# Chunk-selected attention with a routed MoE on one core: Q and K in token order, diagonal tiles masked by fours, SBUF copies by DMA

## The chip, the cores and the metric

One core of a Trainium2 chip runs the whole program in one launch. The metric is device time in microseconds; the kernel before was run three times. The engines are named as in the profile: PE (TensorE matmul), PEld (its weight loads), DVE (VectorE), ACT (ScalarE), POOL (GpSimd), SP (SyncE, which here only issues DMAs).

## What is computed

Attention over 4 batches of 8 heads, 768 tokens, head dimension 64, followed by a mixture of experts over the 3,072 tokens that come out of it. A query sees only six chunks of 32 keys: those with the largest upper bound of its score, which is worked out from the elementwise minimum and maximum of each chunk's keys.

```python
k_min = np.min(k_chunks, axis=3); k_max = np.max(k_chunks, axis=3)
ub = np.sum(np.maximum(q[..., None, :] * k_min, q[..., None, :] * k_max), axis=-1)
ub = np.where(pos[:, None] // chunk >= np.arange(nc)[None, :], ub, -1e9)
top_chunks = np.argsort(ub, axis=-1)[..., -6:]
mask = (key's chunk is in top_chunks) & (pos[:, None] >= pos[None, :])
attn = softmax(where(mask, 0.125 * q @ k.T, -1e9)) @ v
# then, on x = attn as [3072, 512]:
y_dense = relu(x @ w1_dense) @ w2_dense
expert = argmax(x @ w_gate); gate = softmax(x @ w_gate)[expert]
out = y_dense + gate * (relu(x @ w1[expert]) @ w2[expert])
```

All 8 experts have D = F = 512. The inputs are float32; the kernel works in float16 with float32 accumulation.

## The kernel before, in words

**Pairs.** The 32 heads are worked as 16 pairs p of two heads (g = 0, 1), so that the two head dimensions of 64 fill 128 partitions. The token order is interleaved: inside each block of 256 tokens, partition i of slot j holds token 2i + j (the pattern `(T p j) d` in `load`, line 84). So a "tile of 128" holds every second token of a block of 256, and all of K, Q, V and the intermediate x stay in this order.

**Preparation of a pair**, one to three pairs ahead of its use:
- `load` (L84): SP issues two DMAs of 192 KB each for K, Q and V, rows of 512 bytes.
- `cast_qk`, `cast_v` (L351, L352, L358): POOL converts to float16. Q goes into the middle half of a tile `q16` of 256 columns.
- `prep_k`: six PE transposes (L364), ACT copies the result out of PSUM as `kp` (L367), DVE takes for max and min a pairwise operation on the two slots (L372) and a reduction (L373), copies the two halves of `kp` into `kT` of each head (L374, L375), and builds `kb` (L377), the chunk bounds of both heads side by side.
- `prep_q`: six transposes (L384), ACT writes the positive part `qp` (L386), DVE the negative part `qn` (L388).
- `prep_ub`: 13 small matmuls (L393, L397) add up the bounds, twelve MAX8 operations on DVE (L403) find the sixth largest, and one comparison (L405) writes flags of the chunks that were not chosen into the outer columns of `q16`.
- `prep_s(p, g)`: per head six transposes (L411) of Q beside its flags, and a DVE copy (L413). The result `r` has, in 128 rows, the 64 of Q and the flag rows; `kT` has the 64 of K and, in the rows that meet the flags, the constant `exf`, -30000 where a key belongs to that chunk (L129). One score matmul therefore gives q.k plus a large negative number for keys of chunks not chosen.

**Scores and AV.** A head's causal scores are cut into six units of 512 columns (`PIECES`, L180): key tile by query tiles, blocks of 256 tokens on the diagonal kept whole. So a pair has 12 units and 48 tiles of 128 x 128. `scores` runs one or two matmuls (L421), ACT takes the exponential (L425), and POOL sets the entries above the diagonal to zero in the units that touch it (L430, ten of the twelve). `av` multiplies each tile with V and a column of ones (L450); `norm` (L458, L460) divides and writes x into `xbig`.

**Order.** A loop over all (pair, unit) runs scores two units ahead and AV one behind, and at fixed unit numbers the preparation of the following pairs: `prep_s` of the next pair at units 0 and 2, `prep_k` of the one after at 4, `prep_q` at 6, `prep_ub` at 9. Each engine executes its own queue in order; a tile framework inserts the semaphore waits and settles the final order in each queue. From the fifth pair on, the gate, the ranks and the dense layers of the batch before are filled in between (`batch_fills`, L212): transposes of x (L221), gate (L229), dense layers (L299, L308), stores of the dense result to DRAM (L313), of x (L248). POOL also issues the loads of the expert weights (L177) in this loop.

**Routing.** `digits` (L278, L279) writes for each tile of tokens two one-hot matrices, one with the block number of the token and one with its place in it; 48 matmuls (L589) collect them into a list of tokens by expert block. Five small DVE operations turn this into the gather index `gi` and the scatter index `si`. After attention the last batch's dense layers run, and then 31 blocks of 128 tokens: gather by POOL (L625), transposes, two expert layers (L652, L669), scatter (L673).

Of the kernel before, what the change touches and what calls it, by code (L numbers as in the profile page):

```python
# [17 lines left out]
def kernel(  # L18
# [36 lines left out]
    xov = xo.rearrange("(T p j) w -> p T j w", p=128, j=2)  # L55
    NX = 4
    xdv = xd.rearrange("(T p j) w -> p T j w", p=128, j=2)
# [16 lines left out]
    def load(p, names="kqv"):  # L74
        if p >= NP:
            return
        b, hp = divmod(p, HP)
        for nm, src in (("k", k), ("q", q), ("v", v)):
            if nm not in names:
                continue  # L80
            f = aload.tile([128, 2, NT, D], FP, name=nm + "f")
            st[p][nm] = f
            for g in range(2):
                nc.sync.dma_start(out=f[:, g].rearrange("p (T j) d -> p T (j d)", j=NJ),  # L84
                                  in_=src[b, 2 * hp + g].rearrange("(T p j) d -> p T (j d)", p=128, j=NJ))
# [7 lines left out]
    NB = 3  # L93
    kT = [[acst.tile([128, S], HF, name=f"kT{i}_{g}") for g in range(2)] for i in range(NB)]
    q16 = [acst.tile([128, NT, 256], HF, name=f"q16_{i}") for i in range(NB)]
    v16 = [acst.tile([128, 2, NT, D + 1], HF, name=f"v16_{i}") for i in range(NB)]
    for i in range(NB):
        nc.vector.memset(q16[i][:, :, 0:64], 0.0)
        nc.vector.memset(q16[i][:, :, 192:256], 0.0)
# [3 lines left out]
    nc.vector.memset(hmask[0:64, 0, :], 1.0)  # L103
    nc.vector.memset(hmask[64:128, 1, :], 1.0)
    for i in range(NB):
        nc.vector.memset(v16[i][:, :, :, D : D + 1], 1.0)
# [4 lines left out]
    exf = acst.tile([32, S], HF)  # L111
    nc.vector.memset(exf, -30000.0)

    for g in range(2):
        nc.gpsimd.affine_select(out=cbias[:, :, g, :], in_=cbias[:, :, g, :], compare_op=ALU.is_ge,
                                fill=-60000.0, base=0, pattern=[[256, NT2], [1, NJ], [-32, NC]], channel_multiplier=2)
    pat = [[256, NT2], [1, NJ], [2, 128]]
    npat = [[-a, n] for a, n in pat]
    nc.gpsimd.affine_select(out=exf, in_=exf, compare_op=ALU.is_ge, fill=0.0,
                            base=0, pattern=pat, channel_multiplier=-32)  # L120
    nc.gpsimd.affine_select(out=exf, in_=exf, compare_op=ALU.is_ge, fill=0.0,
                            base=31, pattern=npat, channel_multiplier=32)
    for i in range(NB):
        for g in range(2):
            nc.vector.memset(kT[i][g][64 * g : 64 * g + 64], 0.0)

    def expand(i):
        for g in range(2):
            nc.scalar.copy(kT[i][g][64 * g : 64 * g + 32, :], exf)  # L129
# [7 lines left out]
    Am = const.tile([128, NM, 2, 128], HF)  # L137
# [5 lines left out]
    iop = const.tile([128, NJ], FP)  # L143
    xbig = [const.tile([128, NT, XW], HF, name=f"xbig{i}") for i in range(2)]

    def route_consts():
# [11 lines left out]
        nc.gpsimd.iota(iop, pattern=[[1, NJ]], base=0, channel_multiplier=2, allow_small_or_imprecise_dtypes=True)  # L158
# [15 lines left out]
    def load_expert(e, w, behind):  # L174
# [5 lines left out]
    PIECES = [  # L180
        [(0, 0, 512)],
        [(1, 0, 512)],
        [(0, 512, 768), (1, 512, 768)],
        [(2, 256, 768)],
        [(3, 256, 768)],
        [(4, 512, 768), (5, 512, 768)],
    ]
    units = [(g, pc) for g in range(2) for pc in PIECES]
    NU = len(units)
    last_of = {}  # L190
    for u, (g, pc) in enumerate(units):
        for kt, a, z in pc:
            for t in range(a // 128, z // 128):
                last_of[g, t] = (u, kt)

# [16 lines left out]
    def batch_fills(b):  # L212
# [12 lines left out]
        def gate():  # L225
# [20 lines left out]
            for dst in (xov, xdv[:, :, :, 2 * Dm :]):  # L246
                for j in range(NJ):
                    nc.sync.dma_start(out=dst[:, b * NT2 : (b + 1) * NT2, j],  # L248
# [478 lines left out]
```

## Time and profile before

| | |
|---|---|
| median of 3 runs | 308.63 us (308.63, 308.63, 310.03) |
| profiled execution | 308.44 us, its span 306.7 us, granted clock 0.96 |
| start (first V x P matmul with a mask) | about 21.7 us |
| attention, to the last norm | 193.5 us |
| last dense layers and routing | to about 215 us |
| expert blocks | to the end |

A row of the groups reads: line, engine, operation, output and input tile, shapes, count; then the busy time in us and the mean duration of one in ns; then how long the engine stood idle just before, and what ended most of that. Busy time is the union over a group, so that overlapping matmuls are not counted twice. In the slices each digit is the busy share of a fortieth of the span in tenths. The DMA share adds up the time that packets took over 16 DMA engines; it can exceed 1 where packets of several queues overlap.

DMA issues, median from issue to landing: `kf` 4.7 us, `qf` 4.5, `vf` 5.0 (32 DMAs of 192 KB each), the stores of `ys` 3.5 (24 of 256 KB).

### The profile page before, as it was taken

Reading aid. Unit: us, or ns where it says so; the run is one execution under the profiler, and the core shown is the slowest. Engines: PE = TensorE matmul, PEld = TensorE weight load, DVE = VectorE, ACT = ScalarE, POOL = GpSimd, SP = SyncE. Lnnn points to the kernel's source line nnn. Section 1 sums busy time; section 2 is a strip of 40 time slices with the busy share of each in tenths; the row PEclk is TensorE's granted clock in tenths of the full one; section 3 lists DMA queues with packets and bytes.
Section 4 is the critical chain, followed back from the end, with each engine's and each line's share of the span. In section 5 each row is a group of like instructions: output and inputs, shape, how many; then the busy total and the mean of one; then the engine's idle time right before and its main releaser. Section 6 shows DMA issues by size and latency. Waiting matters only on the chain.

```text
span 306.7 us, 7543 instructions
## 1 busy us (share of the span) xinstructions
PE 248.3 (81%) x2607; PEld 154.7 (50%) x2607; DVE 201.2 (66%) x672; ACT 186.9 (61%) x341; POOL 194.1 (63%) x314
## 2 busy tenths in 40 slices
PE   2378877798898879898788899795939999898882
PEld 1246554476565557556566555452425544444440
DVE  6766888779997789996879952591313554443441
ACT  3658888767777987678896778232403554444440
POOL 6667988766656587467776154105764777777752
PEclk9997999989999999999999999999867999999997
DMA  7994997879996998996987821086782777777750
GB/s 198 293 290 129 208 255 147 216 126 186 264 293 162 263 194 175 304 181 157 235 149 116 239 103 70 37 297 186 208 270 93 233 244 249 231 245 255 232 188 0
DMA packets 63478, 60.75 MB, mean 198 GB/s; under 512 B 4494, under 2 KB 56718, under 8 KB 63440
## 3 DMA queue, kind: packets, MB, share of 16 engines
q0 software_dynamic: 15184, 28.60, 41.1%
q1 hardware_dynamic: 48256, 31.66, 35.5%
q8 instruction: 21, 0.34, 0.4%
q14 instruction: 17, 0.14, 0.1%
HBM read 50.62 MB, written 20.91 MB: 233 GB/s over the span
## 4 chain that ended last, share of the span: by engine, by line
PE 31%; DVE 21%; POOL 15%; DMA 12%; issue 11%; ACT 5%; SPq 2%; POOLq 1%; ACTq 0%; DVEq 0%
PE sp L421 6%; DMA xg<-xd,gi 6%; POOL xg L625 4%; PE yp L308 4%; POOL ex L430 4%; PE op L450 4%; PE yp L669 3%; DMA vf<-in_v_dram 3%; ACT ex L425 3%; DVE ks L373 3%; PE hp L652 3%; POOL out_dram L673 3%; PE hp L299 3%; DVE km L372 2%; DVE Am L279 2%
## 5 line engine op out<-in xcount | busy, mean ns | idle before, releaser
L425 ACT ACTIVATE ex<-sp 128x512 f16<-128x512 f32 x192 | 102.9, 613 | 20.4 <-PE sp L421 16.4
L430 POOL TENSOR_SCALAR_AFFINE_SELECT ex<-ex 128x256 f16<-128x256 f16 (+1 forms) x160 | 72.2, 468 | 46.3 <-ACT ex L425 43.4
L421 PE MATMUL sp<-r,kT 128*128 128x512 f16 (+1 forms) x256 | 72.7, 338 | 3.5 <-ACT ex L425 3.1
L450 PE MATMUL op<-v,ex 128*128 128x65 f16 x768 | 59.7, 197 | 6.8 <-POOL ex L430 6.5
L450 PEld LDWEIGHTS <-ex 128*128 128x128 f16 x768 | 46.0, 100 | 38.0 <-POOL ex L430 13.1
L673 POOL DMA_INDIRECT out_dram<-yo,si x31 | 31.4, 1013 | 18.1 <-DVE yo L672 13.2
L663 ACT COPY ehT<-tp 128x512 f16<-128x512 f16 x31 | 18.2, 586 | 37.2 <-PE tp L661 37.2
L646 DVE COPY exT<-tp 128x512 f16<-128x512 f16 x31 | 13.2, 425 | 37.5 <-PE tp L644 37.3
L625 POOL DMA_INDIRECT xg<-xd,gi x31 | 29.9, 963 | 11.4 <-issue 7.3
L652 PE MATMUL hp<-we,exT 128*128 x124 | 33.8, 397 | 3.3 <-issue 3.3
L669 PE MATMUL yp<-we,ehT 128*128 x124 | 33.7, 396 | 0.8 <-ACT ehT L663 0.8
L672 DVE SCALAR_TENSOR_TENSOR yo<-yp,xg 128x512 f32<-128x512 f32 x27 | 20.3, 751 | 13.6 <-PE yp L669 13.2
L655 ACT ACTIVATE eh<-hp 128x512 f16<-128x512 f32 x31 | 18.5, 597 | 15.9 <-PE hp L652 15.9
L299 PE MATMUL hp<-xT,wd 128*128 128x384 f16 x128 | 26.1, 324 | 1.4 <-DVE ys L202 0.3
L301 ACT ACTIVATE hT<-hp 128x384 f16<-128x384 f32 x32 | 15.9, 497 | 17.8 <-PE hp L299 12.0
L421 PEld LDWEIGHTS <-kT 128*128 128x128 f16 x256 | 22.5, 100 | 6.7 <-issue 5.0
L308 PE MATMUL yp<-wd,hT 128*128 128x512 f16 x96 | 25.0, 378 | 0.1
L413 DVE COPY r<-pp 128x768 f16<-128x768 f16 x32 | 16.9, 551 | 8.8 <-PE pp L411 8.7
L403 DVE MAX8 m<-pp 128x8 f32<-128x24 f32 x192 | 20.3, 173 | 3.5 <-PE pp L397 3.4
L358 POOL CAST v<-vf 128x768 f16<-128x768 f32 x16 | 13.4, 840 | 11.3 <-PE op L450 7.8
L367 ACT COPY kp<-pp 128x768 f16<-128x768 f16 x16 | 12.8, 798 | 12.7 <-PE pp L364 12.7
L397 PE MATMUL pp<-kb,qp 128*128 128x48 f16 x96 | 9.4, 187 | 13.3 <-DVE kb L377 13.3
(118 smaller groups left out, 432.7 us busy)
## 6 DMA issues: line engine op xcount, KB each, us to landing
we<-in_moe_w_dram POOLq DMA_DIRECT2D x16, 512.0 KB, 7.9
kf<-in_k_dram SPq DMA_DIRECT2D x32, 192.0 KB, 4.7
qf<-in_q_dram SPq DMA_DIRECT2D x32, 192.0 KB, 4.5
vf<-in_v_dram SPq DMA_DIRECT2D x32, 192.0 KB, 5.0
xd<-ys SPq DMA_DIRECT2D x24, 256.0 KB, 3.5
xo<-xbig SPq DMA_DIRECT2D x8, 396.0 KB, 5.3
xd<-xbig SPq DMA_DIRECT2D x8, 396.0 KB, 6.3
wd<-in_moe_w_dense_dram POOLq DMA_DIRECT2D x2, 512.0 KB, 10.1
```

The lines of the kernel that those rows point to most:

```text
L299: nc.tensor.matmul(hp, wd[:, ko, j * 128 : (j + 1) * 128], xT[:, ko, g * G * 128 : (g + 1) * G * 128], start=(ko == 0), stop=(ko == NK - 1))
L308: nc.tensor.matmul(yp, hold["h"][:, j, i * 128 : (i + 1) * 128], wd[:, NK + j], start=(j == 0), stop=(j == NK - 1))
L403: nc.vector.max(out=m8[:, t, g], in_=ub[:, t, g])
L421: nc.tensor.matmul(sp[:, o : o + z - a], kT[p % NB][g][:, kt * 128 : (kt + 1) * 128], s["r", g][:, a:z], start=(o == 0), stop=True, skip_g ...
L425: nc.scalar.activation(ex, sp, AF.Exp, scale=0.125)
L430: nc.gpsimd.affine_select(out=exd, in_=exd, compare_op=ALU.is_ge, fill=0.0, base=-(pc[0][0] % NJ), pattern=[[-1, n], [1, NJ], [2, 128]], c ...
L450: nc.tensor.matmul(op[:, t * (D + 1) : (t + 1) * (D + 1)], ex[:, c : c + 128], v16[p % NB][:, g, kt, :], start=(first and n == 0), stop=(l ...
L625: nc.gpsimd.indirect_dma_start(out=dst, out_offset=None, in_=src, in_offset=bass.IndirectOffsetOnAxis(ap=gi[:, i : i + 1], axis=0))
L652: nc.tensor.matmul(hp, s["xT"][:, ko], wef[:, bass.ds(offs[i] + ko * 512, 512)], start=(ko == 0), stop=(ko == NK - 1))
L669: nc.tensor.matmul(yp, s["hT"][:, j], wef[:, bass.ds(offs[i] + (NK + j) * 512, 512)], start=(j == 0), stop=(j == NK - 1))
L672: nc.vector.scalar_tensor_tensor(o, yp, s["x"][:, Dm : Dm + 2].bitcast(FP), s["y"], ALU.mult, ALU.add)
L673: sc = nc.gpsimd.indirect_dma_start(out=out, out_offset=bass.IndirectOffsetOnAxis(ap=si[:, i : i + 1], axis=0), in_=o, in_offset=None, bou ...
```

## The change

- **Token order at the transposes.** K is loaded interleaved as before, but ACT's copy after the transposes writes it in token order. Q's transposes write token order inside half-blocks of 64: inside a tile of 128 the even tokens come first, then the odd ones. V is loaded by plain tiles of 128 tokens, in rows of 256 bytes.
- **Units.** A tile of 128 x 128 now covers 128 consecutive keys and queries, so the causal half has 21 tiles a head instead of 24. Units are rebuilt: eleven a pair, of which three consist of four diagonal tiles each, and two have three tiles.
- **Masks.** Only these three units are masked, with one operation of 512 columns each.
- **K and flags.** ACT writes K of both heads straight into `kT[1]`; SP's DMA copies head 0's half into `kT[0]`, and another DMA puts `exf` over the rows it leaves. Flags have tiles of their own (`fl`), one set of six transposes for both heads, one DVE copy `se`, and two DMAs that place 32 rows in each head's `rT`. Q is copied by DVE into `rT[0]` and by DMA into `rT[1]`.
- **Bounds.** The negative part of Q is no longer formed: min(q, 0) k_min is written as q k_min - max(q, 0) k_min, so there are 18 instead of 12 bound matmuls, and `kb` has a third part. MAX8 reads only the causal chunks and skips the first tile.
- **One slot number.** `digits` writes one matrix with one number per token, 24 matmuls instead of 48; `gi` and `si` are worked out from it.
- Stores of x are two a batch instead of four; fills of the ranks come one unit earlier.

```diff
@@ load @@
+                if nm == "v":
+                    nc.sync.dma_start(out=f[:, g], in_=src[b, 2 * hp + g].rearrange("(t p) d -> p t d", p=128))
+                else:
+                    nc.sync.dma_start(out=f[:, g].rearrange("p (T j) d -> p T (j d)", j=NJ),
+                                      in_=src[b, 2 * hp + g].rearrange("(T p j) d -> p T (j d)", p=128, j=NJ))
@@ constants @@
     def expand(i):
-        for g in range(2):
-            nc.scalar.copy(kT[i][g][64 * g : 64 * g + 32, :], exf)
+        nc.scalar.copy(kT[i][0][64:96, :], exf[0:32])
@@ PIECES @@
-        [(0, 0, 512)], [(1, 0, 512)], [(0, 512, 768), (1, 512, 768)],
-        [(2, 256, 768)], [(3, 256, 768)], [(4, 512, 768), (5, 512, 768)],
-    units = [(g, pc) for g in range(2) for pc in PIECES]
+    def of(g):
+        return [
+            [(g, i, i, i + 1) for i in range(4)],
+            [(g, 0, 1, 5)],
+            [(g, 1, 2, 6)],
+            [(g, 2, 3, 6), (g, 4, 5, 6)],
+            [(g, 3, 4, 6), (g, 0, 5, 6)],
+        ]
+    units = of(0) + [[(g, i, i, i + 1) for g in range(2) for i in (4, 5)]] + of(1)
@@ digits @@
-            nc.vector.tensor_scalar(Am[:, m, 0], io128, rf[:, t : t + 1], float(m // NJ + 1), ALU.is_equal, ALU.mult)
-            nc.vector.tensor_scalar(Am[:, m, 1], io128, rf[:, t : t + 1], iop[:, m % NJ : m % NJ + 1], ALU.is_equal, ALU.mult)
+            nc.vector.tensor_scalar(Am[:, m], io128, rf[:, t : t + 1], num[:, m : m + 1], ALU.is_equal, ALU.mult)
@@ prep_k @@
-            kp = ahead.tile([128, S], HF, name="kp")
-            nc.scalar.copy(kp, pk)
+            kp = kT[p % NB][1]
+            nc.scalar.copy(kp.rearrange("d (T p j) -> d T p j", p=128, j=NJ),
+                           pk.rearrange("d (T j p) -> d T p j", p=128, j=NJ))
             for i, op in enumerate((ALU.max, ALU.min)):
-                km = ahead.tile([128, NC, 16], HF, name=f"km{i}")
-                nc.vector.tensor_tensor(km.rearrange("d (T c) w -> d T (c w)", T=NT2), kpv[:, :, 0], kpv[:, :, 1], op)
-                nc.vector.tensor_reduce(out=ks[:, i], in_=km, op=op, axis=mybir.AxisListType.X)
-            nc.vector.tensor_copy(kT[p % NB][0][64:128, :], kp[0:64])
-            nc.vector.tensor_copy(kT[p % NB][1][0:64, :], kp[64:128])
+                nc.vector.tensor_reduce(out=ks[:, i], in_=kp.rearrange("d (c w) -> d c w", w=32), op=op,
+                                        axis=mybir.AxisListType.X)
+            nc.vector.tensor_tensor(kb[:, 2], ks[:, 1:2].to_broadcast([128, 2, NC]), nmask, ALU.mult)
+        def prep_kt(p):
+            k0, k1 = kT[p % NB]
+            nc.sync.dma_start(out=k0[0:64], in_=k1[0:64])
+            nc.sync.dma_start(out=k1[0:32], in_=exf[0:32])
@@ prep_q @@
+            pqv = pq.rearrange("d (T h j p) -> d T h j p", h=2, j=NJ, p=64)
-                nc.tensor.transpose(pq[:, t * 128 : (t + 1) * 128], q16[p % NB][:, t, 64:192], ident)
+                nc.tensor.transpose(pqv[:, t // NJ, :, t % NJ], s["q16"][:, t].rearrange("p g d -> p (g d)"), ident)
-            nc.vector.tensor_single_scalar(qn, pq, 0.0, ALU.min)
+            nc.vector.tensor_copy(r0, pq)
+            nc.sync.dma_start(out=r1[64:128], in_=r0[64:128])
@@ prep_s @@
-                nc.tensor.transpose(ps[:, t * 128 : (t + 1) * 128], q16[p % NB][:, t, g * 128 : (g + 1) * 128], ident)
-            s["r", g] = r = ahead.tile([128, S], HF, name=f"r{g}")
-            nc.vector.tensor_copy(r, ps)
+                nc.tensor.transpose(ps[:, t * 128 : (t + 1) * 128], fl[p % 2][:, t], ident)
+            nc.vector.tensor_copy(se, ps)
+            nc.sync.dma_start(out=r0[64:96], in_=se[64:96])
+            nc.sync.dma_start(out=r1[0:32], in_=se[0:32])
@@ scores @@
-            n = sum(a == (kt // NJ) * 256 for kt, a, z in pc)
-            if n:
-                exd = ex[:, 0 : n * 256]
-                nc.gpsimd.affine_select(out=exd, in_=exd, compare_op=ALU.is_ge, fill=0.0, base=-(pc[0][0] % NJ),
-                                        pattern=[[-1, n], [1, NJ], [2, 128]], channel_multiplier=-2)
+            nc.scalar.activation(ex[:, 0:o], sp[:, 0:o], AF.Exp, scale=0.125)
+            if pc[0][1] == pc[0][2]:
+                nc.gpsimd.affine_select(out=ex, in_=ex, compare_op=ALU.is_ge, fill=0.0, base=0,
+                                        pattern=[[0, 4], [1, 2], [2, 64]], channel_multiplier=-1)
@@ the loop @@
-            if u == 0 and n1 is not None:
-                prep_s(n1, 0)
             if u == 2 and n1 is not None:
-                prep_s(n1, 1)
+                prep_s(n1)
             if u == 4 and n2 is not None:
                 prep_k(n2)
-            if u == 6 and n2 is not None:
+            if u == 5 and n2 is not None:
                 prep_q(n2)
+            if u == 7 and n2 is not None:
+                prep_kt(n2)
@@ routing @@
-            for i in range(2):
-                nc.tensor.matmul(pm[:, i], Am[:, m, i], eqb[:, m], start=(m == 0 and i == 0), stop=(m == NM - 1),
-                                 skip_group_check=True)
+            nc.tensor.matmul(pm, Am[:, m], eqb[:, m], start=(m == 0), stop=(m == NM - 1))
```

At the start the three `expand` copies now come before everything else of ACT; before, one came first and the rest after the first pair's preparation. In the changed kernel the copies of L397 and L398 (K), L410 (Q), L438 and L439 (flags) are the new DMAs on SP's queue, L448 the scores, L467 the AV matmuls and L454 the masks.

## The prediction

> **What bounds it now.** I read the busy row, the slices, the windows of the attention stage, its groups, its waits, and last the DMA of the start, in that order.
>
> ```profile
> PE 248.3 (81%) x2607; PEld 154.7 (50%) x2607; DVE 201.2 (66%) x672; ACT 186.9 (61%) x341; POOL 194.1 (63%) x314
> ...
> PE   2378877798898879898788899795939999898882
> ...
> DVE  6766888779997789996879952591313554443441
> ...
> DMA  7994997879996998996987821086782777777750
> ...
> PE 31%; DVE 21%; POOL 15%; DMA 12%; issue 11%; ACT 5%; SPq 2%; POOLq 1%; ACTq 0%; DVEq 0%
> ```
>
> One slice is 7.7 us. Attention fills slices 3 to 25, the experts' stage the last twelve. The change touches the first 215 us alone. No engine is full there, and the chain of the last end changes hands between PE, DVE and POOL: a pipeline of nearly equal engines. Windows inside it (columns: length, PE, PEld, DVE, ACT, POOL busy, clock, DMA share):
>
> ```profile
> 25.00:62.00 37.00, 28.92 (x388) 19.87 (x386) 29.12 (x97) 29.34 (x55) 30.52 (x56) 0.96 0.89 184
> 62.00:160.00 98.00, 87.09 (x1118) 60.45 (x1117) 84.04 (x312) 76.76 (x146) 66.14 (x122) 0.99 0.92 208
> 160.00:193.00 33.00, 29.98 (x351) 19.23 (x350) 22.21 (x88) 24.63 (x49) 15.48 (x33) 1.00 0.52 130
> sum 168.00, PE 145.99 PEld 99.55 DVE 135.38 ACT 130.73 POOL 112.14; mean PE 48.66 PEld 33.18 DVE 45.12 ACT 43.58 POOL 37.38
> ```
>
> In the middle window PE is busy 89%, DVE 86%, and the DMA engines 0.92. There a pair of heads takes 11.2 us (K casts of POOL L351 start at 56.47 and, eight pairs on, at 146.03). Groups of 25 to 193 us:
>
> ```profile
> L425 ACT ACTIVATE ex<-sp 128x512 f16<-128x512 f32 x184 | 98.7, 613 | 18.5 <-PE sp L421 14.5 <-PE op L450 2.0 <-POOL ex L430 1.4
> L430 POOL TENSOR_SCALAR_AFFINE_SELECT ex<-ex 128x256 f16<-128x256 f16 x122 | 50.3, 422 | 33.2 <-ACT ex L425 31.9
> ...
> L450 PEld LDWEIGHTS <-ex 128*128 128x128 f16 x739 | 44.0, 99 | 33.9 <-POOL ex L430 10.6 <-issue 9.3 <-ACT ex L425 0.2
> ...
> L430 POOL TENSOR_SCALAR_AFFINE_SELECT ex<-ex 128x512 f16<-128x512 f16 x31 | 20.2, 653 | 12.3 <-ACT ex L425 10.8 <-DMA xd<-ys 0.6
> ...
> L373 DVE TENSOR_REDUCE ks<-km 128x24 f16<-128x384 f16 x28 | 14.0, 541 | 0.0
> ...
> L375 DVE COPY kT<-kp 64x768 f16<-64x768 f16 x14 | 7.1, 507 | 0.2
> ```
>
> The reader is to see that PE waits 10.6 us for masks of POOL. A second wait of PE, for `kb` at L397 (13.3 us, 13 times), ends a DVE chain that the change rewrites.
>
> ```profile
> q1 hardware_dynamic: 10413, 5.12, 99.5%
> ...
> kf<-in_k_dram SPq DMA_DIRECT2D x10, 192.0 KB, 4.8
> ```
>
> This is the DMA of the first 20 us: SP's queue keeps all 16 engines full. 0.995 x 20 us x 16 / 10,413 is 30.6 ns for a packet of 512 bytes.
>
> **The Trainium skill.** "VectorE: DVE Perf Modes", section "The perf-mode tier table": a tensor_reduce has only the one-element-a-cycle mode, at 0.96 GHz. The trace agrees: 384 elements take 541 ns, 400 of them elements, so 768 should take 941 (an estimate). "SBUF — State Buffer", section "SBUF: two separate sides": DVE and GpSimd lock a port pair from each other for a whole instruction. The trace fits: one `digits` operation (L279) took 1.90 us at 131.05, while POOL issued weights and ran masks, 0.31 us at 201 with POOL idle. "DMA: Bandwidth & Descriptors", section "Why small descriptors are slow (HBM only)": 3 cycles of overhead a packet, so 256 bytes cost 11 where 512 would cost 19; its Specifications name 512 bytes as the least for full rate. No packet of 256 bytes can be singled out here. Same page, "Queues, rings and completion order": a ring's descriptors are taken in order. So a small copy on SP's ring lands behind the loads ahead of it; landings in this trace (loads 2.3 to 9.9 us, median near 5; `ys` writes 2.0 to 7.8) are the price.
>
> **The change, step by step.** Whole-kernel counts; the sum is made against the profiled execution, 308.44 us (span 306.7), 0.19 under the median 308.63.
>
> Step 1, PE. Scores shrink from 6,144 to 5,376 columns a pair; four matmuls of 512 run in 0.86 us at L652, 0.42 ns a column: 16 x 768 x 0.42 = -5.2 us. AV matmuls 768 to 672 at 29 ns (four in 0.28 us, one 0.193): -2.8. Flag transposes 192 to 96 at 55 ns (twelve in 0.83 us): -5.3. Bound matmuls 192 to 288 at 25 ns (twelve in 0.3 us at 127.7): +2.4. Net -10.9. The Q transpose's split output I take at nothing (no row; 0 to +1 us in all).
>
> Step 2, DVE. Two `kT` copies gone, -15.2 (6.9 + 8.3). Pairwise max/min gone and reductions doubled: -13.0 + 32 x 0.40 = -0.2. Second `kb`: +16 x 0.3 = +4.8, priced as the first without contention. One flag copy of two gone: -8.5. MAX8 192 at 106 ns to 160 that are 8 columns narrower on average, 98 ns: -4.6. `digits` one of two gone, 18 before 193 us: -5.8. Net -29.5 of 135. This goes beside PE work; its worth is that PE's partners are no longer level with it. The chain from ACT's K copy to `kb` stays near 3 us (1.9 reductions, 0.55 copy, 0.7 `kb`, against 3.2 at 124.57 to 127.66), so the 13.3 us wait stays.
>
> Step 3, ACT and POOL. Exponentials 192 to 176, 32 of them of 384 columns (116 ns less, L301's 497 against 613): -12.3 of ACT. Masks 160 to 48, all of the 653 ns form: 72.2 to 31.3, -40.9 of POOL. ACT's K copy now reorders: 0 to 0.8 us each, I take 0 (same element count). Of PE's 10.6 us of waits for masks seven tenths could go, 7.4; many end with an exponential just behind, so I take -3 (0 to -7.4).
>
> Step 4, copies by DMA: five a pair on SP's queue, 344 KB, 80 in all at about 0.5 us of issue (loads' median 0.486). Per pair SP then issues 11 to 13 for about 6 us, plus one wait: `exf` into `kT` (L398) waits for the landing of the K copy just before it, and behind it stand the Q and V loads and the flag copies L438, L439. K copies are issued a pair early; loads are two pairs ahead. The flag copies are the only urgent ones: in the built order about 6.5 us of PE work lie between the flag transposes and the next pair's first score; transposing and DVE's copy take 1, so issue and landing have 5.5. With 0.5 + 4.7 they just fit, and a slower landing is late by what it exceeds. I take 0.2 us a pair, +3 in 15 pairs (0 to +8). ACT's K copy and DVE's flag copy wait for landings of two or three pairs before, long past: nothing.
>
> Step 5, V by 128 tokens: packets of 256 bytes, 1,536 a pair for 768. 17.7 ns (the page's 11/19) to 30.6: +0.23 to +1.47 us of all engines a pair, and the copies +1.2 at the start's 290 GB/s. On 10.3 us of DMA work a pair (0.92 x 11.2) that makes 11.7 to 13.0. If share meant capacity this would bind. But two queues overlap in it (the 10 to 20 us window reads 1.17, slices at 120 us reached 378 GB/s). I count nothing, and keep the rest for a rival.
>
> Step 6, start. First score now at 16.36. Two more ACT copies of `exf` lie ahead of the K copy (0.83 each): +1.7. DVE to `kb` -0.6, MAX8 -0.2, six transposes fewer and one copy fewer -1.25. Flag copy: 0.5 + 4.8 = +5.3. First score near 21.3, +4.9. But POOL's first mask waits today until 21.2 behind casts that wait for V's load; mask to mask the loss is 1.3. I take +3.
>
> Step 7, after attention. 24 of 48 slot matmuls gone (1.36 us at 205): -0.7 on a full PE; last unit needs no mask (0.65): -0.6; six `digits` operations fewer, beside PE work: -0.2. Together -1.5. Slot numbers' extra small DVE operations on `si` are hidden behind gathers; without cover 0.7. Merged `xo`/`xd` stores move the same bytes: 0.
>
> Sum: -10.9 - 3 + 3 + 3 - 1.5 = -9.4, so 299.0.
>
> **Rivals.** A, the sum: 299.0, own range 293 to 305.
>
> B, the loosened pipeline: all lose at least what ACT loses (9.4%), and the coupling gives PE's idle back. 168 x 9.4% = -15.8, start +0, tail -2: 290.6. For it, POOL and DVE fall by 36% and 22%. Against it, the `kb` wait stays.
>
> C, late flag copies (slower): place L438/L439, PE's first scores of a pair. Landing at 7.5 us, as loads took in the 60 to 100 us stretch (medians 8.7 to 8.8 for K and V), gives 0.5 + 7.5 - 5.5 = 2.5 late; PE is in order, so AV behind it stands too: 15 x 2.5 = +37.5 at worst. It decides from 12.4 / 15 = 0.83 us a pair (what A leaves without its +3). With half of it, 1.5 us a pair, 308.4 - 12.4 + 22.5 = 318.5. Against it: ys writes land in a median of 3.5.
>
> D, DMA engines full: middle pairs run at 11.7 instead of 11.2 for eight pairs, +4, beside half of A's gain elsewhere, -4.5: 308. For it 0.92 and late `kf`; against it the peaks of 378 GB/s.
>
> That the change does not do what it says is excluded for counts: the built order holds 48 masks and 176 exponentials.
>
> **Numbers.** Chances A 0.60, B 0.15, C 0.15, D 0.10. Under half a per cent (1.5 us) a measurement of this kernel can't tell from no change. Faster: A but 0.02, B: 0.73. Same: 0.02 + half of D, 0.07. Slower: 0.20. Range: B's 290.6 less 1.6 for its tail, to 312, about D with V's packets between their two prices (12.35 - 11.2 is 1.15 us in eight pairs, so 308.4 + 9.2 - 4.5 = 313), leaving C's bulk and a little of B and D out: 289 to 312.
>
> **What would show it.** Step 1: PE busy of the attention stage near 135. Step 2: DVE near 106; reductions near 941 ns. Step 3: PE's waits for masks down by over half. Step 4: waits of PE at the score line for DMA `se` under 5 us; over 12 means C. Step 5: V landings near 6 us, POOL's casts not waiting for loads; otherwise D. Step 6: first masked AV 23 to 25 us. Wrong altogether if attention's last norm comes later than 193.5 us.

## The result, and the profile after

The changed kernel takes 339.7 us (four runs, 339.02 to 342.63), the kernel before 309.33 (four runs beside it, 308.63 to 310.11): 1.0999 times the time, with a 95% interval of 1.0923 to 1.1075. The prediction, 299.0 us with a range of 289 to 312, was wrong, and on the wrong side. The profiled execution took 339.06 us (span 337.3). Executions of a kernel fall into a faster and a slower state; the ratios below are of the fast ones, the times in us are medians of all, and the traces of e8, e15 and e17 are of slow executions, so that their last norms lie somewhat late.

First the page of the kernel after: busy row, slices (one is now 8.4 us), and the chain by engine and by line.

```profile
PE 244.4 (72%) x2615; PEld 156.8 (46%) x2615; DVE 165.7 (49%) x556; ACT 173.6 (51%) x322; POOL 154.0 (46%) x203
...
PE   1418727849949859686686696989874998899882
...
DMA  7976989797998798899994897223869578877760
...
DMA 38%; PE 31%; issue 8%; DVE 8%; POOL 6%; ACT 4%; SPq 3%; POOLq 1%; ACTq 0%; DVEq 0%
DMA rT<-se 24%; PE sp L448 10%; DMA xg<-xd,gi 9%; PE yp L326 6%; POOL xg L647 3%; ACT ex L452 3%; DMA kT<-kT 3%; PE hp L317 3%; PE op L467 2%; POOL out_dram L695 2%; PE yp L691 2%; SPq L88 2%; PE hp L674 2%; PE pp L434 1%; DVE ks L388 1%
```

DVE has lost 35 us of work and POOL 40, as intended. Yet a quarter of the chain of the last end is one kind of DMA, the flag copies `rT<-se`, and PE's row has holes (1, 2, 4, 5) all through attention. Its windows (columns: length, PE, PEld, DVE, ACT, POOL busy, clock, DMA share, GB/s):

```profile
25.00:62.00 37.00, 24.15 (x337) 18.45 (x336) 18.39 (x74) 22.31 (x43) 16.50 (x23) 0.83 0.84 177
62.00:160.00 98.00, 74.38 (x972) 52.99 (x969) 57.12 (x212) 61.51 (x120) 39.29 (x55) 0.87 0.93 209
160.00:225.00 65.00, 50.48 (x604) 34.24 (x605) 30.55 (x118) 38.98 (x78) 19.21 (x28) 0.89 0.72 167
sum 200.00, PE 149.01 PEld 105.67 DVE 106.07 ACT 122.80 POOL 75.00; mean PE 49.67 PEld 35.23 DVE 35.36 ACT 40.93 POOL 25.00
```

In the middle window PE is busy 76% where it was 89. The waits (engine, line, waited for: us in all, times, longest):

```profile
PE sp L448 <- DMA rT<-se: 45.7, 13, 7.3
DVE se L436 <- PE pp L434: 37.3, 13, 7.6
...
POOL q L371 <- DMA qf<-in_q_dram: 19.0, 7, 5.7
...
PEld L467 <- POOL ex L454: 4.2, 5, 2.2
...
PE op L467 <- POOL ex L454: 3.0, 4, 1.9
...
PE pp L420 <- DVE kb L391: 2.8, 2, 2.0
```

The waits for masks have fallen by more than half and those for `kb` have almost gone; a wait of 45.7 us for the flag copies has come. By stage: the last norm starts at 227.2 us instead of 193.8 (+33.4); what follows it is 2.9 us shorter (337.3 - 227.2 against 306.7 - 193.8).

One pair shows the mechanism. PE (start, length, line; in brackets idle time before, and what ended it):

```profile
102.31 0.85 PE L434 MATMUL pp<-ident,fl 128*128 128x128 f16 x6
...
111.18 0.38 PE L448 MATMUL sp<-rT,kT 128*128 128x128 f16 x4 [0.83 <-DMA rT<-se]
```

DVE copied the flags at 103.19 (0.56 us), so they lay ready at 103.75. SP in the same stretch (a row with x2 runs from the start of the first issue to the end of the second):

```profile
103.45 0.55 SPq L398 DMA_DIRECT2D kT<-exf  x1
104.05 0.58 SPq L88 DMA_DIRECT2D qf<-in_q_dram  x1
104.73 0.90 SPq L331 DMA_DIRECT2D xd<-ys  x2
105.69 1.08 SPq L86 DMA_DIRECT2D vf<-in_v_dram  x2
106.86 0.57 SPq L438 DMA_DIRECT2D rT<-se  x1
107.48 0.60 SPq L439 DMA_DIRECT2D rT<-se  x1
```

The copies stand behind six other issues and are both out only at 108.08, 4.3 us after the flags were ready; PE's first score comes 3.1 us later. Until 103.45 SP itself had waited at L398 for the landing of the K copy L397, as it does in other pairs:

```profile
SPq L398 <- DMA kT<-kT: 26.6, 12, 5.2
```

In this pair PE stood for 0.83 us only. Over the twelve pairs after the first in which PE waited: flags ready to both issued 4.25 us, issued to first score 4.21, against 5.24 us between flags ready and PE falling idle. So each is 3.2 us late. Of the 4.25, 1.60 pass before the first of the two is issued, 1.83 are that issue itself, and 0.77 the second: the issue takes as long as the queue ahead of it.

### The profile page after: what moved, and what is told of

It is laid out like the page before. It is cut to its first block, busy times and chain, and to the rows that moved or that the text cites. A ratio compares the mean times of both kernels' runs of the same rounds, so it can differ in the third digit from the quotient of the medians.

```text
span 337.3 us, 7413 instructions
## 1 busy us (share of the span) xinstructions
PE 244.4 (72%) x2615; PEld 156.8 (46%) x2615; DVE 165.7 (49%) x556; ACT 173.6 (51%) x322; POOL 154.0 (46%) x203
## 3 DMA queue, kind: packets, MB, share of 16 engines
q1 hardware_dynamic: 65280, 37.17, 40.2%
## 4 chain that ended last, share of the span: by engine, by line
DMA 38%; PE 31%; issue 8%; DVE 8%; POOL 6%; ACT 4%; SPq 3%; POOLq 1%; ACTq 0%; DVEq 0%
DMA rT<-se 24%; PE sp L448 10%; DMA xg<-xd,gi 9%; PE yp L326 6%; POOL xg L647 3%; ACT ex L452 3%; DMA kT<-kT 3%; PE hp L317 3%; PE op L467 2%; POOL out_dram L695 2%; PE yp L691 2%; SPq L88 2%; PE hp L674 2%; PE pp L434 1%; DVE ks L388 1%
## 5 line engine op out<-in xcount | busy, mean ns | idle before, releaser
L452 ACT ACTIVATE ex<-sp 128x512 f16<-128x512 f32 (+1 forms) x176 | 92.6, 591 | 66.3 <-PE sp L448 63.0
L448 PE MATMUL sp<-rT,kT 128*128 128x128 f16 (+3 forms) x384 | 72.3, 297 | 46.8 <-DMA rT<-se 45.7
L454 POOL TENSOR_SCALAR_AFFINE_SELECT ex<-ex 128x512 f16<-128x512 f16 x48 | 31.8, 665 | 84.1 <-ACT ex L452 83.8
L448 PEld LDWEIGHTS <-kT 128*128 128x128 f16 x384 | 32.0, 109 | 56.3 <-issue 50.9
L467 PE MATMUL op<-v,ex 128*128 128x65 f16 x672 | 52.2, 201 | 8.0 <-ACT ex L452 4.7
L467 PEld LDWEIGHTS <-ex 128*128 128x128 f16 x672 | 39.7, 103 | 24.0 <-ACT ex L452 8.5
L388 DVE TENSOR_REDUCE ks<-kT 128x24 f16<-128x768 f16 x32 | 29.1, 947 | 14.7 <-ACT kT L384 13.9
L674 PE MATMUL hp<-we,exT 128*128 x124 | 31.8, 379 | 4.6 <-DVE exT L668 3.3
L426 DVE MAX8 m<-pp 128x8 f32<-128x8 f32 (+4 forms) x160 | 16.0, 167 | 29.1 <-PE pp L420 28.9
L668 DVE COPY exT<-tp 128x512 f16<-128x512 f16 x31 | 13.1, 424 | 33.3 <-PE tp L666 33.3
L436 DVE COPY se<-pp 128x768 f16<-128x768 f16 x16 | 8.9, 557 | 37.3 <-PE pp L434 37.3
L371 POOL CAST q<-qf 128x768 f16<-128x768 f32 x16 | 13.2, 824 | 25.9 <-DMA qf<-in_q_dram 19.0
```

The source lines that it names most:

```text
L388: nc.vector.tensor_reduce(out=ks[:, i], in_=kp.rearrange("d (c w) -> d c w", w=32), op=op, axis=mybir.AxisListType.X)
L448: nc.tensor.matmul(sp[:, o : o + w], kT[p % NB][g][:, kt * 128 : (kt + 1) * 128], rT[p % NB][g][:, a * 128 : z * 128], start=(o == 0), sto ...
L452: nc.scalar.activation(ex[:, 0:o], sp[:, 0:o], AF.Exp, scale=0.125)
L454: nc.gpsimd.affine_select(out=ex, in_=ex, compare_op=ALU.is_ge, fill=0.0, base=0, pattern=[[0, 4], [1, 2], [2, 64]], channel_multiplier=-1)
L467: nc.tensor.matmul(s["op", g][:, t * (D + 1) : (t + 1) * (D + 1)], ex[:, o : o + 128], v16[p % NB][:, g, kt, :], start=first, stop=(last_o ...
L674: nc.tensor.matmul(hp, s["xT"][:, ko], wef[:, bass.ds(offs[i] + ko * 512, 512)], start=(ko == 0), stop=(ko == NK - 1))
```

## The experiments

The theory after the result was: the flag copies are the cost, because PE, which is in order, meets them before they land (the expectations call this the theory of the lead; the lead is the time that PE has other work to do). The rivals: the copies are late only through their place in SP's queue; small packets and copies fill the DMA engines; and copies cost without being waited for, through traffic or SP's time. Each kernel is compared with the kernel before on its own chip. From `e9` on the chips were others, on which the kernel before took 329 to 330 us; for the kernel without copies by DMA the excess lies after attention (its last norm starts at 178.5 us on one chip and 178.4 on another, at 291.87 and 306.52 us in all). So ratios and last norms are compared there, not times.

| kernel | SBUF copies by DMA, a pair | us | ratio to before (95%) | last norm starts |
|---|---|---|---|---|
| before | none | 309.33 | 1 | 193.8 |
| changed | K 2, Q 1, flags 2 | 339.70 | 1.0999 (1.0923-1.1075) | 227.2 |
| e1 | K 2, Q 1 | 314.39 | 1.0223 (1.0123-1.0322) | 200.8 |
| e2 | all, flags on ACT's queue | 342.65 | 1.1089 (1.0993-1.1186) | 231.2 |
| e3 | all, V in 512 bytes | 334.14 | 1.0769 (1.0622-1.0916) | 221.6 |
| e4 | Q 1, flags 2 | 332.11 | 1.0725 (1.0638-1.0812) | 217.8 |
| e5 | none | 291.87 | 0.9441 (0.9352-0.9529) | 178.5 |
| e6 | all, flags earlier in the source | 335.06 | not given | 220.9 |
| e7 | K 2 | 305.37 | 0.9868 (0.9757-0.9980) | 190.2 |
| e8 | flags 2 | 329.10 | 1.0619 (1.0526-1.0712) | 218.3 |
| e13 | none (e5 again) | 306.52 | 0.9347 (0.9268-0.9427) | 178.4 |
| e15 | none, five unread | 329.90 | 0.9997 (0.9957-1.0038) | 198.5 |
| e14 | none, five unread from a constant | 337.42 | 1.0267 (1.0134-1.0400) | 206.8 |
| e16 | none, five unread of a quarter | 330.29 | 1.0016 (0.9983-1.0048) | 201.4 |
| e17 | none, one unread of all bytes | 318.35 | 0.9507 (0.9375-0.9639) | 189.5 |

**Flags without a DMA (e1).**

```diff
-            nc.vector.tensor_copy(se, ps)
-            nc.sync.dma_start(out=r0[64:96], in_=se[64:96])
-            nc.sync.dma_start(out=r1[0:32], in_=se[0:32])
+            nc.vector.tensor_copy(r0[64:96], ps[64:96])
+            nc.vector.tensor_copy(r1[0:32], ps[0:32])
```

> The changed kernel with one edit: DVE writes the flag rows of both heads straight out of PSUM (two copies of 32 rows, about 0.55 us each) instead of one copy and two DMAs; K and Q copies stay on DMA. Late flag copies (theory 1): the 45.7 us that PE waits for se at the score line go, 0.55 us of DVE a pair comes, attention's last norm falls from about 227 to 190 to 195 us and the time to 300 to 306. Full DMA engines (theory 2): flags were 98 of 344 KB of copies a pair and no V packet is changed, so the casts' waits for loads take over and the time stays above 325. SP's queue (theory 3, head of line): waits of casts for loads stay at 15 to 25 us, since L398 still waits for L397 ahead of the Q loads; time 310 to 325.

314.39 us: 25 us back, half of the way to none. That is above the 300 to 306 of late flags alone and inside the 310 to 325 given for SP's queue, but the sign named for that, POOL's casts waiting 15 to 25 us for loads, is not there (9.8 us). Its waits name another reason:

```profile
DVE rT L436 <- DMA rT<-rT: 42.0, 10, 8.7
```

DVE's write of the flags now waits for the landing of the Q copy L410, which reads the rows that the flags go into. A second copy costs as well once the first is gone; e7, which takes it away too, is 9.0 us faster.

**The flag copies from another queue (e2).** L438 and L439 issued by `nc.scalar` instead of `nc.sync`.

> The changed kernel with the two flag DMAs issued from ACT's queue, everything else the same bytes. If the flags are late because they stand behind V's loads and the wait of L398 on SP's queue and ring (theory 1 in its ring form, or 3), landings fall from a median of 5.4 us to 2 to 3.5 and the waits of PE for se from 45.7 us to under 20: time 312 to 325, with about 1 us a pair of ACT issue as its price. If the DMA engines are full (theory 2), landings stay at 5 us and the time at 335 or more.

342.65 us, no gain. Over twelve pairs ready to issued is 3.06 us on ACT's queue, issued to score 3.78, against 2.86 until PE is idle: 4.0 late. The three longest delays before the issue, 4.6, 5.5 and 7.6 us, ended with the landing of the Q copy L410, which reads rows that the flag copy writes: ACT stood idle for it. A place out of SP's queue does not help by itself, since the copy still depends on one from there, and since the built order put the transposes nearer to their reader (PE is busy for 3.5 us between the last flag transpose and the pair's first score, for 5.0 in the changed kernel). The median landing is 5.4 us from either queue. Time and landing are what full DMA engines were expected to give; but from 60 to 140 us the DMA share is 0.86 here, and it was 0.93 in the kernel before.

**V in rows of 512 bytes (e3).** V is loaded with the pattern of K, so each key meets another key's V.

> The changed kernel with V loaded as before, in rows of 512 bytes; V's rows then stand in another order than the keys, so the output is not the reference's, the amount of work is the same. Full DMA engines through small packets (theory 2): V's landing falls, the flags' landing with it (they follow V on the ring), waits of PE for se fall by half or more, time 315 to 325. Lead too short and ring order as such (theory 1): 384 KB still lie ahead of the flags, landing falls by at most 1 us, time 330 to 337.

334.14 us: 5.6 less than the changed kernel, and the intervals of the two ratios just fail to touch. PE still waits 42.6 us for the flags (45.7), nearer to what was given for the lead than for full engines. But V's rows bear on SP's queue: from 60 to 140 us an issue of a flag copy takes 0.65 us on average where it took 1.17, and POOL's wait for the Q loads falls from 19.0 us to 1.4. That PE waits nearly as long goes with a shorter lead: it is busy for 4.0 us between the last flag transpose and the pair's first score, 5.0 in the changed kernel.

**No copy by DMA at all (e5).** K goes from ACT into a tile `kp` and by two DVE copies into `kT`, the chunk rows are written once, Q's second head and the flags by DVE from PSUM.

```diff
-            nc.sync.dma_start(out=k0[0:64], in_=k1[0:64])
-            nc.sync.dma_start(out=k1[0:32], in_=exf[0:32])
+            nc.vector.tensor_copy(k0[0:64], st[p]["kp"][0:64])
+            nc.vector.tensor_copy(k1[64:128], st[p]["kp"][64:128])
...
-            nc.sync.dma_start(out=r1[64:128], in_=r0[64:128])
+            nc.vector.tensor_copy(r1[64:128], pq[64:128])
```

> The changed kernel with none of its five SBUF copies by DMA: ACT writes K to a tile of its own and DVE makes the two K copies (0.43 and 0.52 us, as the kernel before), DVE writes head 1's Q (0.55 us) and both flag rows (2 x 0.55 us) from PSUM; exf is written once at the start. DVE gains about 2.0 us a pair over the changed kernel, ending near 138 us in the attention stage, as before. Theory 1 alone: as the flags-by-DVE kernel or 0 to 8 us slower through DVE, 300 to 312. Theory 3: faster than the flags-by-DVE kernel by 5 us or more, because loads no longer wait behind L397 and L398. The trimming alone (steps 1 and 3 of the prediction) is then worth 3 to 12 us against before.

291.87 us, the fastest: below the 300 to 312 that late flags alone would give, and more than 5 us below e1, as the theory of SP's queue had it. It is 47.8 us under the changed kernel and 17.9 under the kernel before. Its windows:

```profile
25.00:62.00 37.00, 29.80 (x480) 22.36 (x481) 35.61 (x115) 31.64 (x61) 25.60 (x36) 1.00 1.04 209
62.00:160.00 98.00, 88.09 (x1191) 62.21 (x1190) 88.15 (x307) 71.82 (x143) 44.98 (x62) 0.97 1.06 233
160.00:178.00 18.00, 17.49 (x207) 11.23 (x206) 10.82 (x36) 14.59 (x30) 3.92 (x6) 1.00 0.17 63
sum 153.00, PE 135.38 PEld 95.80 DVE 134.58 ACT 118.05 POOL 74.50; mean PE 45.13 PEld 31.93 DVE 44.86 ACT 39.35 POOL 24.83
```

DVE carries the copies (199.5 us busy in the whole kernel against 165.7) and is at 90% in the middle, PE too. All else of the change together is a gain; the five copies by DMA, against copies by DVE, cost 47.8 us.

**One kind of copy at a time (e4, e7, e8).** The same edits, for K alone (e4), for Q and flags (e7), for K and Q (e8).

> K of both heads is put into kT by two DVE copies (32 more of about 0.5 us), the chunk rows are written once; the Q copy and the two flag copies stay DMAs on SP's queue. So L398, which waits at the head of SP's queue for the landing of L397, is gone, and 48 of the 80 copies remain. Theory of the lead (each flag copy lands about 5 us after its issue, and PE has less than that to do): PE's waits for the flag copies stay at 35 us or more, time 330 to 338. Rival, the head of the queue (the flag copies are late because they are issued late, behind L398): waits under 20 us, time 312 to 320.

> Only the two copies of K and of the chunk rows (L397, L398) stay DMAs; the Q copy is a second DVE copy out of PSUM, and the flags are written by DVE straight into rT. Between the kernel with the flags on DVE alone (314.4) and the one with no copies by DMA (291.9). Theory of the lead: the K copies are issued a pair ahead of their reader, so they cost little, and the Q copy was what held that kernel: 294 to 300. Rival, the head of SP's queue (L398 waits for L397, and K, Q and V loads behind it come late): 306 to 314, with POOL waiting for DMA qf.

> K and Q copies by engines; only the two flag copies a pair (L438, L439) are DMAs, with nothing but loads on SP's queue. Theory of the lead: they still land 4 to 5 us after issue and PE has no more to do than before, so PE's waits for them are 20 us or more and the time is 308 to 320 (against 291.9 with none). Rival, the copies hold each other up (five together): landing under 3 us, waits under 10, time 292 to 299.

Over the 291.87 of none, K by DMA costs 13.5 us, the flags 37.2, flags and Q 40.2, K and Q 22.5 (e1), all 47.8: not a sum, since one wait hides another. In e4 PE waits 37.4 us for the flags though L397 and L398 are gone, as the theory of the lead had it; in e8, whose time lies above the 308 to 320 given for it, 34.6. In both the queue is short: flags ready to both issued takes 2.5 and 2.4 us (means of the pairs in which PE waited), issued to score 3.9 and 3.7. But PE now falls idle 3.3 and 2.9 us after the flags are ready, where it was 5.24, so the copies are again 3.1 us late. In the built order it is busy for 3.9 and 3.8 us between the last flag transpose and the pair's first score, for 5.0 in the changed kernel. A shorter queue alone did not cure them, because the lead shrank too. e7's 305.37 us fell between the two ranges given for it, and its waits name a reason that neither had:

```profile
PE sp L446 <- DMA kT<-kT: 9.8, 5, 3.8
...
PE sp L446 <- DMA kT<-exf: 8.8, 4, 3.7
```

The K copies, taken as not urgent, are waited for by PE as well.

**More lead (e6, e9, e12).** e6: the flag transposes at unit 0 instead of 2.

> The changed kernel with the flag transposes, DVE's copy and the two flag DMAs of the next pair two units earlier in the order (at unit 0 instead of 2); all five copies stay DMAs. Theory of the lead: two units are about 2.2 us of the pair's 13, so each of 13 waits of 3.5 us shrinks by about 2: PE's waits for the flag copies near 20 us, time 312 to 320. Rival, full DMA engines (copies finish when the bytes ahead of them are through, and work put earlier only waits longer): waits stay above 35 us, time above 332.

335.06 us, waits 41.2: the numbers that were given for full DMA engines. But it did not test what it was meant to: between the last flag transpose and the pair's first score PE is busy for 4.7 us a pair in its trace, and for 5.0 in that of the changed kernel. The framework settles the order and did not keep the distance of the source. e9 and e12 take the kernel e8 and copy the flags of the pair before, which are ready a pair earlier (the queries then see chunks chosen for another pair, with the same work). The edit of e12:

```diff
             if u == 9 and n2 is not None:
                 prep_ub(n2)
+                put_flags(n1, n2)
```

> As the kernel in which only the two flag copies a pair are DMAs (329.1 us, 37 more than with no copies by DMA), but each pair takes the flags of the pair before it: the same 32 DMAs of 48 KB carry them a pair earlier than their reader needs them. Queries therefore see chunks chosen for another pair of heads; the work is the same. Theory of the lead (what costs is only that PE stands in line for a copy that is not there): PE's waits for the flag copies under 5 us, time 291 to 300. Rival, traffic or SP's queue (the copies cost by what they take from the DMA engines and from the loads behind them): time above 315 whatever PE waits for.

> The early flags mended: in the kernel with flags a pair early PE waited for the copies at the bound matmuls (35 us at L423), since these read the rows that the flag copy writes. Here the copy of the flags of the pair before is put behind the bound matmuls of the next pair, so that about a pair lies between it and its reader; chunks again chosen for another pair of heads. Theory of the lead: PE's waits for flag copies under 8 us, time 0.95 to 0.98 of the kernel before. Rival, SP's queue and traffic: 1.03 or more, whatever PE waits for.

e9 (360.9 us, 1.1053, interval 1.0915 to 1.1191) moved the wait: its copy stood ahead of the bound matmuls, which read the whole of `r0`.

```profile
PEld L423 <- DMA rT<-se: 35.6, 11, 7.3
```

e12, where it stands behind them (the diff above), gave 1.0249 (1.0138 to 1.0360), last norm 205.3 against e8's 218.3, and PE still waited 27.0 us for flags: the copy must now wait until the bound matmuls have read `r0`, and between the last of these and the pair's first score PE is busy for only 2.1 to 7.0 us. No run here gave the flag copies a longer lead; whether that would have cured it stays open.

**Copies that nobody reads (e11, e15, e14).** The kernel without copies by DMA, and beside it the five copies of the changed kernel, at its places on SP's queue, into a tile that is never read (e11, and e15 on the same chip as e13); in e14 they all read a constant tile, so that none waits for a producer. PE, ACT and POOL execute the same instructions in the same order in all of them as in e5, and DVE has at most a memset more.

> As the kernel with no copies by DMA (291.87 us), and beside it the same five SBUF copies a pair as in the changed kernel, 344 KB on SP's queue at the same places, into a tile that nobody reads. The output is the reference's computation unchanged. Theory of the lead (copies cost what somebody waits for, not what they move): 292 to 299. Rival, traffic and SP's queue (80 more issues, 5.5 MB more, loads behind them late): above 310, with POOL waiting for the loads of Q and V.

> The kernel with no copies by DMA once more, because the three kernels before this one were run on a chip on which the kernel before took 329 us, and have to be compared with it on one chip. Both theories: 0.935 to 0.953 of the kernel before.

> The five unread copies beside the kernel with no copies by DMA, once more, on the same chip as that. After the first run (1.0043 of the kernel before, against 0.944 without them on another chip) the theory of the lead alone expects what it expected, 0.95 to 0.97; the theory that copies cost through SP's queue and the DMA engines too, so that loads come late, expects 0.99 to 1.02.

> The same five unread copies a pair, of the same sizes at the same places on SP's queue, but all read from one constant tile: none has to wait at the head of the queue for a producer. If the copies cost by waiting at the head of SP's queue with loads behind them: 0.94 to 0.96 of the kernel before, and POOL's waits for loads as without copies. If they cost by bytes, packets and issue time: as the unread copies, 0.99 to 1.02.

e11: 1.0043 (0.9968 to 1.0118); e15: 0.9997 against e13's 0.9347. So copies whose results nobody reads cost 6.5% of the kernel before, and 20 us of last norm (198.5 against 178.4). The theory of the lead alone falls. Nor is it waiting at the head of the queue for a producer: without producers it costs more (e14: 1.0267, above both ranges given, last norm 206.8). SP in e14:

```profile
104.97 1.29 SPq L88 DMA_DIRECT2D qf<-in_q_dram  x2
106.30 1.21 SPq L447 DMA_DIRECT2D du<-zc  x1
107.55 0.59 SPq L448 DMA_DIRECT2D du<-zc  x1
108.24 2.07 SPq L86 DMA_DIRECT2D vf<-in_v_dram  x2
110.36 1.85 SPq L419 DMA_DIRECT2D du<-zc  x1
```

Line upon line, hardly a gap. Of the 80 us from 60 to 140 SP is issuing for 71.8 here (83 issues, 0.87 each), 68.8 in e15 (85), 57.2 in the changed kernel (77, 0.74 each), 33.5 in the kernel before (53, 0.63 each), 32.8 in e5 (54). The 81.5 in the expectation of e16, more than the window holds, takes in time between issues. What comes late is the loads:

```profile
POOL k L374 <- DMA kf<-in_k_dram: 28.4, 8, 7.2
```

They are late in the queue more than on the way. K's loads have two buffers, so a pair's load may be issued when the cast of two pairs before is done. In e13 SP waits for that cast:

```profile
SPq L88 <- POOL k L371: 9.9, 6, 2.8
```

There the issue comes 0.2 us after the cast (median of eight middle pairs, K), as in the kernel before; 14.2 us after it in e14, 11.1 in e15, and 15.5 in the changed kernel. From issue to landing K takes 6.3 us in e14 and 4.8 in e13 (medians from 60 to 140 us).

**Issues or bytes (e16, e17).** e16 takes e14's five copies at a quarter of the length, e17 all the bytes as one copy.

```diff
-            nc.sync.dma_start(out=du[p % NB][0:64, 0], in_=zc[0:64])
+            nc.sync.dma_start(out=du[p % NB][0:64, 0, 0:192], in_=zc[0:64, 0:192])
```

> The kernel with no copies by DMA, and beside it 80 unread copies from a constant tile, each a quarter as long as in the run with full ones (86 KB a pair instead of 344). In that run SP was issuing for 81.5 of the 80 us from 60 to 140, 0.95 us an issue. If the number of issues costs (SP's queue full, loads behind it late): 0.99 to 1.03 of the kernel before, attention's last norm after 195 us. If the bytes cost (DMA engines full): 0.94 to 0.96, last norm before 186.

> The same 344 KB a pair of unread bytes, but as one copy of 128 rows instead of five, 16 issues in place of 80. If the number of issues costs: 0.94 to 0.96 of the kernel before, last norm before 186 us. If the bytes cost: 0.99 to 1.03, last norm after 195.

e16: 1.0016, last norm 201.4. Against e14, whose copies it shortens, a quarter of the bytes saves 5.4 us of attention (the intervals of the two ratios are apart) and leaves 23.0 of the 28.4 that the copies cost over e13. e17, on the same chip as e16: 0.9507, last norm 189.5 (above the 186 given; the traced execution, 320.26 us, is the longest of its four): all the bytes in one issue cost 11 us over e13. So the number of copies is the larger part, and the bytes are not free (in e17 61 issues take 59.9 of the 80 us, 0.98 each, in e16 91 take 66.5, 0.73 each). K's loads are issued 12.4 us after the cast in e16 and 7.3 in e17. In e16 the DMA share from 60 to 140 us is 0.92, below the 1.06 of e13: full DMA engines are not the reason there. e17 also has fewer packets (2,304 for the copies, where e14 and e16 have 4,864), so that issues and packets are not told apart by these two.

**Two more on the kernel without copies (e10, e18).** K's copies by POOL instead of DVE, and V in 512 bytes.

> As the kernel with no copies by DMA (291.87 us), the two copies of K a pair (L400, L401) by POOL instead of DVE. DVE is busy 88 to 93 per cent of 25 to 140 us there, POOL about half. If DVE is the bound, 32 copies of about 0.5 us off it give 286 to 291; rival: POOL takes longer for a copy than DVE did and holds up masks and casts behind it: 292 to 300.

> The kernel with no copies by DMA, with V loaded in rows of 512 bytes, its rows in another order (each key meets another key's V). With the copies this was worth 5.6 us (339.7 to 334.1). If the DMA engines still bound the kernel without copies (share above 1 up to 140 us): 3 to 8 us less, 0.91 to 0.935 of the kernel before on a chip where it is 0.935 to 0.944 with rows of 256 bytes. If they do not: within 2 us of it.

e10: 306.09 us, 0.9354 (0.9231 to 0.9478), no different from e13; its last norm came 4.8 us sooner (173.6), the end did not, and why stays open. e18: 0.9244 (0.9117 to 0.9372), 1% under e13, but the intervals overlap: small packets may cost some 3 us there, not settled.

## Why the prediction was wrong, point by point

**Step 1 (PE) was right.** PE's 135 us is what the kernel without copies has (135.38). In the changed kernel the same matmuls take 149.01, at a granted clock of 0.83 to 0.89 in place of 0.97 to 1.00.

**Step 2 (DVE) was right in size**: 106.07 us for 106, a reduction 947 ns for 941. Its last sentence was wrong: the 13.3 us of waits for `kb` did not stay (2.8). It is 2.4 in e5 as well, where DVE is as busy as before, so DVE's relief is not what removed it; what did is open.

**Step 3 (masks) was right**: 48 masks take 31.8 us for 31.3, and PE's and PEld's waits for them are 3.0 and 4.2 where those of the whole kernel before were 6.5 and 13.1.

**Step 4 (five copies by DMA) is the step that failed.** "With 0.5 + 4.7 they just fit" into 5.5 us. The lead was nearly right (5.24), and the landing too: from the start of the second issue to the score 4.98 us for 4.7. The 0.5 was wrong: from flags ready to both copies issued took 4.25 us. It holds one issue where there are two (0.77 for the second), leaves out what stands in SP's queue ahead of them (1.60), and takes an issue at its median of 0.486 us, where the first of the two took 1.83. The mean of all issues from 60 to 140 us, which decides how fast a queue drains, was 0.63 in the kernel before (33.5 us for 53 issues) and is 0.74 after. The "about 6 us" of issue a pair are 9.3 of 13 us (57.2 of 80). The step also took the other copies as not urgent. L398, which it knew to wait for L397's landing, holds up what is behind it; e1 shows the Q copy waited for by DVE once the flags are gone, e7 the K copies by PE. And it counted only copies that are late, where even unread ones cost 20 us of attention: K's loads are issued 11.1 us after their buffer is free (e15) and not 0.2 (e13). The landing, which the step priced by the loads ahead on SP's ring, had the same median of 5.4 us from ACT's queue (e2). The step was taken as +3; the copies measured 47.8. The prediction's own signs said as much: the waits for `se` were to stay under 5 us and are 45.7, the last norm was not to come after 193.5 and comes at 227.2.

**Step 5 (V's packets)** was counted at nothing; e3 puts it at 5.6 us with the copies there, and part of it sits in step 4's issues (1.17 us a flag copy, 0.65 with rows of 512 bytes). Of the two prices the low one, an estimate of 17.7 ns a packet of 256 bytes, was nearly right: they took 19.3 ns on average from 60 to 140 us, those of 512 bytes 29.7. V's landing has a median of 5.3 us for the 6 forecast. POOL's casts do wait for loads (19.0 us for Q), which by the step's own sign means full DMA engines; but these loads are issued 18.0 us after their buffer is free (median of eight middle pairs, 0.0 before), so the sign can't tell engines from queue.

**Step 6 (start)** was too small. The first masked AV came at 26.29 us for 23 to 25. The flags were ready at 15.56, but L398 stood at the head of SP's queue, L438 was issued at 21.05, and the first score came at 23.91: 8.35 us where the step had 0.5 + 4.8.

**Step 7 (tail)**: -2.9 for -1.5.

**Rivals.** C was right in the place and in what PE does there, and its worst case was too small: 3.2 us late in twelve pairs and 7.0 at the start, for 2.5 in fifteen. What makes the copies late it had wrong: it feared landings of 7.5 us, and the issue was what was long. It got 0.15, on the ground that `ys` writes land in 3.5 us. B's number is that of the change without the copies, 291.87 us for its 290.6, but not its ground: DVE, whose relief was to loosen the pipeline, is as busy there as before (199.5 us for 201.2), while POOL is relieved (155.1 for 194.1) and the `kb` wait, its counter-argument, is gone. Which of these counts was not tested, so the near hit may be luck. D, full DMA engines, has a part in V's small packets (e3), but is not the main cost: the changed kernel's DMA share is lower than that of e5, which is 47.8 us faster (0.93 against 1.06 in the middle window), and copies of a quarter of the bytes keep 23.0 us of 28.4.

## What to carry to other kernels

A small copy moved from an engine to a DMA queue costs issue time on an in-order queue, and its reader gets it after queue, issue and landing. Add up the queue from the mean issue time of the stretch, count every issue ahead of the copy, and set that against the lead of the built order, which has to be read again after every edit (5.24 us in the changed kernel, 2.9 in e2 and e8). If the queue also carries the loads, count every issue as time taken from them, even if no one waits for the copy.

## What was not expected of the hardware

- The issue of a small SBUF copy on SP took from 0.53 to 4.92 us (L438, median 0.80), and 83 issues took 71.8 of 80 us (e14). With V in rows of 512 bytes the flag copies' issues took 0.65 on average for 1.17 (e3, 60 to 140 us), and on ACT's queue the issue of L438 took 0.51 to 0.65 (e2). What else stretches them was not tested.
- Bytes mattered less than the number of copies: with 12 and 24 KB the last norm came at 201.4 us (e16), with 48 and 96 KB at 206.8 (e14), with all bytes in one copy at 189.5 (e17), with none at 178.4 (e13).
- PE's idle time came with a lower granted clock, 0.87 in the middle window against 0.97 in the kernel without the copies, and with longer matmuls (score matmuls 297 ns against 260). That the waits bring this about was not tested; if they do, part of each is paid for twice.
